# A convolution and gated feed-forward kernel: the opening's filter band, convolution order and two requests for x rearranged

## The chip, the core and the metric

The kernel runs on one core of a Trainium2 chip. A core has a matrix engine (TensorE, PE in the profile; its weight loads have rows of their own, PEld), a vector engine (VectorE, DVE), a scalar engine (ScalarE, ACT), a general engine (GpSimd, POOL) and a sync engine (SyncE, SP), which here issues transfers only. Each runs its own stream of instructions in order, and they meet at semaphores. TensorE writes its products into an accumulation memory, PSUM, in banks of 512 float32 columns; VectorE and ScalarE bring them from there to the working memory. The metric is device time in microseconds (us) for one execution.

## The reference

```python
def _attn_ref(x, weight):                       # x: 8 x 4096 x 192, weight: 8 heads x 7 taps
    w = np.exp(weight - np.max(weight, axis=-1, keepdims=True))
    w = w / (np.sum(w, axis=-1, keepdims=True) + 1e-09)
    x_pad = np.concatenate([np.zeros((B, pad, D)), x], axis=1)      # 6 zero rows in front
    ...
    out = np.einsum('hk,bskhg->bshg', w, x_unf)   # each head's 24 columns, 7 rows back
def _moe_ref(x, w_gate, w_val, w_out):          # 192 -> 1536 -> 192, on 32768 rows
    gate = np.maximum(x @ w_gate, 0.0)
    val = x @ w_val
    return gate * val @ w_out
```

A causal convolution over the sequence, with seven softmax taps per head, feeds a feed-forward layer whose hidden vector is the product of a rectified gate and a value.

## The kernel before

The 32768 rows are two streams of four sequences each, carried side by side. A unit is 2 x 512 rows of both streams, and there are 16 units. For each unit, `gate_val` (matmuls at L621) multiplies the convolved rows (`xc`, columns in three chunks `c` of 64) with `Wg` and `Wv` in twelve blocks `f` of 128 hidden columns; ScalarE rectifies the gate (L632) and VectorE multiplies by the value (L633). `project_turn` (L643) multiplies with `Wo`. From unit 1 on the convolution is done tap by tap on ScalarE, VectorE and GpSimd, a unit ahead. The first windows cannot wait for that, so the opening convolves them on TensorE with a band matrix. The order of every engine's stream is the order in which the code is written.

This opening is what the change touches. In the order of the code:

- `hold` (L193) issues matmuls of constant ones into the PSUM tile `held`; their results are not used. `WARM` gives their lengths in units of 128 columns: four at the start, three after the small matmul that spreads the taps (L203).
- The filter band. `spread` gets the taps, ScalarE and VectorE form the softmax, and VectorE writes `blocks` at L299: one scaled 22-column block for each of the 8 heads, in three instructions for heads 0 to 2, 3 to 5 and 6 to 7 (the three `BANDS`). TensorE (L335) places eight shifted copies of the blocks into PSUM with the shift matrix `Z`, eight matmuls for each band, all accumulating on zeros that L209 wrote there. VectorE casts the three bands to `band0`, `band3`, `band6` (L343). The third band's PSUM home is the second bank of `held`.
- Meanwhile the five steps of the first x window (`raw`, five transfers) are cast on ScalarE (L119), in the order `STEPS0` = 1, 0, 2, 3, 4.
- The first convolution (`conv_steps`, L391): for each chunk `c` and each step eight small matmuls in four 32-column tiles of the array, 120 in all, into three PSUM tiles `first[0..2]`. Chunk 0 reads `band0`, chunk 1 `band0` and `band3`, chunk 2 `band3` and `band6`.
- `evict` (L402) casts each chunk's 512 columns into `xc`: chunk 0 and 2 on ScalarE, chunk 1 on VectorE. `both_halves` (L231) copies a 128-column piece of a weight to the other 64 partitions: pieces 0 and 1 on VectorE, pieces 2 to 9 on GpSimd (`pool_halves`, a `Wg` and a `Wv` copy for each), piece 10 by transfer.
- GpSimd's stream also issues the transfers of the weights (L224) and of x. The x of the second window (`load_x(1, ...)`, L97) is asked for one stream at a time: stream 0 after piece 2, stream 1 after piece 5. It is used by `conv_steps(1, ...)` in block `f` = 10 of the first window.

Of the kernel before, what the change touches and what calls it, by code (L numbers as in the profile page):

```python
# [11 lines left out]
ALU = mybir.AluOpType  # L12
# [3 lines left out]
def kernel(  # L16
# [12 lines left out]
    nc = tc.nc  # L29

    B, S, D = x.shape
    H, KW = weight.shape
# [7 lines left out]
    WIN = 512  # L40
    NWIN = S // WIN
    SUB = 112
    STEP = 106
    STEPS = [6, 5, 2]
    TAPS = [(6, 5), (4, 3), (2, 1, 0)]
    GSUB = 5
    WARM = [(4, 4, 4, 1), (4, 4, 1)]
    STEPS0 = [1, 0, 2, 3, 4]
    CONV1 = 10


# [29 lines left out]
    def staged(i, j):  # L81
        return stages[i][:, XH * j : XH * (j + 1)]

    def load_x(g, streams=range(2)):


        bp, toks = GROUPS[g]
        xt = staged(g // 3, g % 3).rearrange("p (j s d) -> p j s d", s=2, d=D)
        step = toks[1] - toks[0]
        rows = -(-(step + PAD) // 16) * 16  # L90
        for st in streams:
            src = bass.AP(
                tensor=x.tensor,
                offset=x.offset + ((bp + NB * st) * S + toks[0] - PAD) * D,
                ap=[[D, rows], [step * D, len(toks)], [1, D]],
            )
            nc.gpsimd.dma_start(out=xt[0:rows, 0 : len(toks), st, :], in_=src)  # L97
        return xt

    xts = {0: staged(0, 0).rearrange("p (j s d) -> p j s d", s=2, d=D)}  # L100
# [56 lines left out]
    Z = const.tile([128, 256], F16)  # L157
    nc.gpsimd.memset(Z[:], 0.0)
    nc.gpsimd.memset(raw[0][0:PAD, :], 0.0)
    mask = const.tile([128, H, 1], FP)  # L160
    with nc.allow_low_precision("one of the terms is not zero"):
        nc.vector.tensor_reduce(
            out=Z[:, 112 : 112 + HR],
            in_=eye[:].rearrange("p (g i) -> p i g", i=HR),
# [4 lines left out]
        out=mask[:, :, 0],  # L169
        in_=eye[:].rearrange("p (g i) -> p g i", i=HR),  # L170
# [17 lines left out]
    def many(n):  # L188
        return bass.AP(tensor=one.tensor, offset=one.offset, ap=[one.ap[0], [0, n]])

    def hold(*counts):
        for reps in counts:
            nc.tensor.matmul(  # L193
                out=held[:, 0, 0 : 128 * reps],
                lhsT=many(128),
                rhs=many(128 * reps),
                start=True,
                stop=True,
            )

    spread = psum.tile([128, 2, 512], FP, name="ps")
    hold(*WARM[0])
    nc.tensor.matmul(out=spread[:, 0, 0:KW], lhsT=rows8[:], rhs=w8[:], start=True, stop=True)  # L203
# [25 lines left out]
    def both_halves(copy, s, dst):  # L229
        cols = slice(HALVES[s], HALVES[s + 1])  # L230
        copy(out=dst[64:128, :, cols], in_=dst[0:64, :, cols])  # L231
# [39 lines left out]
    for s in range(2):  # L271
# [4 lines left out]
        out=mx[:], in_=spread[:, 0, 0:KW], axis=mybir.AxisListType.X, op=ALU.max, negate=True  # L276
    )
    nc.scalar.activation(out=e[:, 0:KW], in_=spread[:, 0, 0:KW], func=ACTF.Exp, bias=mx[:])
    sm = const.tile([128, 1], FP)
    total = const.tile([128, KW + 1], FP)  # L280
    nc.scalar.activation(out=total[:], in_=e[:], func=ACTF.Copy, accum_out=sm[:])
    for jj in STEPS0[:3]:
        cast(nc.scalar.copy, jj)
# [4 lines left out]
        out=prod[:],  # L288
        in0=bass.AP(tensor=z0.tensor, offset=z0.offset, ap=[z0.ap[0], [1, BW], [1, KW]]),
        in1=bass.AP(tensor=e0.tensor, offset=e0.offset, ap=[e0.ap[0], [0, BW], [1, KW]]),  # L290
        op=ALU.mult,
    )
    blk = const.tile([128, 1, BW], FP)
    nc.vector.tensor_reduce(out=blk[:, 0, :], in_=prod[:], axis=mybir.AxisListType.X, op=ALU.add)
    nc.vector.reciprocal(sm[:], sm[:])
    blocks = const.tile([128, H, BW], F16)
    for heads in BANDS:
        n = len(heads)
        nc.vector.scalar_tensor_tensor(  # L299
            out=blocks[:, heads[0] : heads[0] + n, :],  # L300
            in0=blk[:].to_broadcast([128, n, BW]),
            scalar=sm[:],
            in1=mask[:, heads[0] : heads[0] + n, :].to_broadcast([128, n, BW]),
            op0=ALU.mult,
            op1=ALU.mult,
        )
# [4 lines left out]
    for s in range(2, 4):  # L311
        load_w(s)
    pool_halves(2)
    xts[1] = load_x(1, range(1))
    for s in (3, 4, 5):
        pool_halves(s)
    load_x(1, range(1, 2))
    for s in (6, 7):
        pool_halves(s)
# [3 lines left out]
    lane_load(0, range(1, 2))  # L323
    for jj in STEPS0[3:]:
        cast(nc.scalar.copy, jj)

    bands = [const.tile([128, len(heads), SUB], F16, name=f"band{heads[0]}") for heads in BANDS]
    for part, heads, to, copy in zip(
        raised, BANDS, bands, [nc.vector.tensor_copy] * 3
    ):  # L330
        n = len(heads)
        for j in range(128 // HR):
            s0 = HR * j - PAD
            lo, hi = max(0, -s0), min(BW, SUB - s0)
            nc.tensor.matmul(  # L335
                out=part[:, 0 : SUB * n].rearrange("p (h t) -> p h t", t=SUB)[:, :, s0 + lo : s0 + hi],
                lhsT=Z[:, 112 - HR * j : 240 - HR * j],
                rhs=blocks[:, heads[0] : heads[0] + n, lo:hi],
                start=False,
                stop=(j == 128 // HR - 1),  # L340
                skip_group_check=True,
            )
        copy(out=to[:].rearrange("p h t -> p (h t)"), in_=part[:, 0 : SUB * n])  # L343

    tap = const.tile([128, NCH, KW], FP)

    for c in range(NCH):
        r0 = 0
        while r0 < 64:
            h = (64 * c + r0) // G  # L350
            r1 = min(64, G * (h + 1) - 64 * c)
            row = wn[HR * h : HR * h + 8, :]
            for st in range(2):
                nc.sync.dma_start(
                    out=tap[64 * st + r0 : 64 * st + r1, c, :],
                    in_=bass.AP(
                        tensor=row.tensor,
                        offset=row.offset,
                        ap=[row.ap[0], [0, (r1 - r0) // 8], [1, KW]],
                    ),  # L360
# [6 lines left out]
    def band(h):  # L367
        return bands[h // 3][0 : SUB + PAD, h % 3, :]

    dense, xcs = {}, {}  # L370
# [6 lines left out]
    def conv_steps(g, ps, c, steps):  # L377


        for jj in steps:  # L380
            col = STEP * jj
            n = min(STEP, WIN - col)
            rows = n + PAD
            for second in range(2):
                for st in range(2):
                    for k2 in range(2):
                        k = 2 * c + k2
                        h0, h1 = 32 * k // G, (32 * k + 31) // G
                        h, m = (h0, G * h1 - 32 * k) if second else (h1, 32)
                        p0 = 64 * st + 32 * k2  # L390
                        nc.tensor.matmul(  # L391
                            out=ps[p0 : p0 + m, 0, col : col + n],
                            lhsT=xts[g][0:rows, jj, st, 32 * k : 32 * k + m],
                            rhs=band(h)[0:rows, 0:n],
                            start=True,
                            stop=True,
                            tile_position=(0, p0),
                            skip_group_check=True,
                        )

    def evict(copy, g, ps, c):
        copy(out=dense[0][:, g, c, :], in_=ps[:, 0, :])  # L402

    def conv(g):

# [301 lines left out]

    dense[0] = xcpool.tile([128, 2, NCH, WIN], F16, name="xc")
    first = [psum.tile([128, 2, 512], FP, name="ps") for _ in range(NCH)]
    for c, steps in ((0, STEPS0[:3]), (1, STEPS0[:2]), (0, STEPS0[3:]), (1, STEPS0[2:]), (2, STEPS0)):  # L710
        conv_steps(0, first[c], c, steps)
    both_halves(nc.vector.tensor_copy, 0, Wg)
    both_halves(nc.vector.tensor_copy, 0, Wv)
    for c, copy in enumerate((nc.scalar.copy, nc.vector.tensor_copy, nc.scalar.copy)):
        evict(copy, 0, first[c], c)
    both_halves(nc.vector.tensor_copy, 1, Wg)
    both_halves(nc.vector.tensor_copy, 1, Wv)
    xts[2] = load_x(2)
# [3 lines left out]
        out=plain.rearrange("p (c d) -> p c d", d=D), in_=moe_w_out.rearrange("(c p) d -> p c d", p=128)  # L722
# [78 lines left out]
```

## Time and profile before

| | |
|---|---|
| three timed runs | 761.57, 761.65, 763.04 us; median 761.65 |
| span of the profiled execution, first to last instruction | 760.2 us |
| TensorE busy | 756.0 us, 99% of the span |
| VectorE, ScalarE, GpSimd busy | 89%, 80%, 61% |
| first matmul of L621 | 7.81 us after the start |

The profiled execution has no time of its own in the list beside its span; against the median of the three runs, 1.4 us lie outside the span, before the first and after the last instruction. Rows of the profile give start and duration in us, then engine, line, operation, tile written and tiles read. A matmul's row is longer than the time after which the next can follow, since matmuls are pipelined. A number `x24` counts instructions that follow each other in one row, whose duration then runs from the first start to the last end.

### The profile page before, as it was taken

The page shows a single profiled execution, that of the slowest core. Times are in us where ns is not written, and L with a number is a line of the kernel's source. Part 1 is how long each engine was busy: PE and PEld are TensorE (multiplying, and loading weights), DVE is VectorE, ACT ScalarE, POOL GpSimd, SP SyncE. Part 2 cuts the span into 40 slices and gives each one's busy share as a digit, 9 for nine tenths or more (in the row PEclk, how much of TensorE's full clock was granted, in tenths as well). Part 3 has the DMA queues.
Part 4 walks back from the last instruction along what each step waited for, and adds up shares of the span by engine and source line. Part 5 has one row for each costly group of instructions (what it writes and reads, how often), then busy time and mean ns, then how long its engine had stood idle before and what let it go on. Part 6 is the DMA issues. An engine that isn't in the chain of part 4 may idle for free.

```text
span 760.2 us, 30531 instructions
## 1 busy us (share of the span) xinstructions
PE 756.0 (99%) x13724; PEld 454.8 (60%) x13724; DVE 675.8 (89%) x647; ACT 610.1 (80%) x680; POOL 461.3 (61%) x311
## 2 busy tenths in 40 slices
PE   9999999999999999999999999999999999999998
PEld 5555555565565666656666565666656556566658
DVE  7889989998998989989999899998999989897891
ACT  7897887878878788887877878788797887877671
POOL 8729649195591946829377392874919659193600
PEclk9999999999999999999999999999999999999999
DMA  8953532345324443333434324352243531240302
GB/s 142 137 69 92 79 85 46 43 96 75 85 44 52 97 66 85 55 61 83 60 85 71 66 67 55 85 85 69 56 49 93 77 86 44 23 100 9 85 2 85
DMA packets 153714, 54.07 MB, mean 71 GB/s; under 512 B 148912, under 2 KB 153584, under 8 KB 153584
## 3 DMA queue, kind: packets, MB, share of 16 engines
q1 hardware_dynamic: 117376, 37.78, 21.6%
q0 software_dynamic: 35808, 14.07, 16.4%
q8 instruction: 107, 1.75, 1.0%
q10 hardware_dynamic: 400, 0.27, 0.1%
q14 instruction: 23, 0.19, 0.1%
HBM read 28.98 MB, written 25.17 MB: 71 GB/s over the span
## 4 chain that ended last, share of the span: by engine, by line
PE 99%; DMA 0%; ACT 0%; issue 0%
PE ps L621 65%; PE ps L643 31%; PE ps L686 2%; PE ps L391 0%; DMA w<-in_weight_dram 0%; PE ps L193 0%; PE ps L335 0%; PE ps L414 0%; PE ps L209 0%; PE ps L203 0%; ACT out_s L697 0%; ACT L127 0%
## 5 line engine op out<-in xcount | busy, mean ns | idle before, releaser
L633 DVE TENSOR_TENSOR hT<-gr,ps 128x1024 f16<-128x1024 f16 (+1 forms) x385 | 469.1, 1219 | 35.5 <-ACT gr L632 8.7
L632 ACT ACTIVATE gr<-ps 128x1024 f16<-128x1024 f32 (+1 forms) x385 | 392.8, 1021 | 114.4 <-PE ps L621 114.4
L550 POOL TENSOR_TENSOR prod<-prod,prod 128x896 f32<-128x896 f32 x145 | 302.6, 2087 | 251.8 <-DVE prod L584 242.7
L621 PE MATMUL ps<-xc,Wg 64*64 64x512 f16 (+1 forms) x4464 | 318.4, 376 | 0.0
L621 PE MATMUL ps<-xc,Wv 64*64 64x512 f16 (+1 forms) x4464 | 318.3, 376 | 0.0
L643 PE MATMUL ps<-hT,Wo 64*64 64x512 f16 x4320 | 235.8, 376 | 0.0
L621 PEld LDWEIGHTS <-Wv 64*64 64x64 f16 (+1 forms) x4464 | 149.9, 106 | 98.5 <-DVE hT L633 0.3
L621 PEld LDWEIGHTS <-Wg 64*64 64x64 f16 (+1 forms) x4464 | 145.4, 107 | 103.4 <-issue 0.2
L643 PEld LDWEIGHTS <-Wo 64*64 64x64 f16 x4320 | 137.3, 107 | 95.7
L538 ACT ACTIVATE prod<-x_r,tap 128x1024 f32<-128x1024 f16 (+2 forms) x195 | 182.7, 1017 | 0.0
L574 DVE SCALAR_TENSOR_TENSOR acc<-x_r,tap,acc 128x1024 f32<-128x1024 f16 (+3 forms) x150 | 118.0, 854 | 0.0
L661 DVE STREAM_TRANSPOSE out_s<-ps 128x1024 f32<-128x1024 f32 x45 | 56.2, 1248 | 28.4 <-PE ps L643 24.4
L550 POOL TENSOR_TENSOR xc<-prod,prod 128x896 f16<-128x896 f32 x29 | 60.6, 2089 | 2.3
L479 POOL COPY x_p<-x_e 128x1536 f16<-128x1536 f16 (+1 forms) x32 | 42.2, 1351 | 0.0
L251 POOL DMA_DIRECT2D x_e<-in_x_dram x30 | 26.6, 890 | 0.0
L574 DVE SCALAR_TENSOR_TENSOR xc<-x_r,tap,acc 128x1024 f16<-128x1024 f16 (+3 forms) x30 | 25.2, 840 | 0.0
L563 ACT ACTIVATE acc<-x_r,tap 128x1024 f32<-128x1024 f16 (+3 forms) x30 | 22.5, 800 | 0.0
L656 ACT COPY turned_by<-ps 128x2 f32<-128x2 f32 x45 | 7.0, 155 | 16.8 <-PE ps L643 14.8
L686 PEld LDWEIGHTS <-hT 128*128 128x128 f16 x192 | 15.8, 98 | 0.4 <-issue 0.4
L686 PE MATMUL ps<-Wo,hT 128*128 128x192 f16 x192 | 16.0, 246 | 0.0
L697 ACT COPY out_s<-ps 128x768 f32<-128x768 f32 (+2 forms) x5 | 3.2, 638 | 12.7 <-PE ps L686 12.7
L697 DVE COPY out_s<-ps 128x192 f32<-128x192 f32 x1 | 0.4, 359 | 13.3 <-PE ps L686 13.3
(61 smaller groups left out, 74.4 us busy)
## 6 DMA issues: line engine op xcount, KB each, us to landing
out_dram<-out_s SPq DMA_DIRECT2D x125, 192.0 KB
x_e<-in_x_dram POOLq DMA_DIRECT2D x28, 384.0 KB, 6.3
x_r<-x_p SPq DMA_TRANSPOSE x116
prod<-in_moe_w_out_dram POOLq DMA_DIRECT2D x1, 576.0 KB, 8.7
prod<-in_x_dram SPq DMA_DIRECT2D x3, 168.0 KB
out_dram<-out_s SPq DMA_DIRECT2D x5, 96.0 KB
out_s<-in_x_dram POOLq DMA_DIRECT2D x2, 210.0 KB, 6.2
out_s<-in_x_dram POOLq DMA_DIRECT2D x2, 192.0 KB, 6.1
```

Source lines behind the costliest of these rows:

```text
L251: nc.gpsimd.dma_start(out=xe[:, 0:n, st, :, :].rearrange("p j c r -> p j (c r)"), in_=bass.AP(tensor=x.tensor, offset=x.offset + row * D, ...
L479: nc.gpsimd.tensor_copy(out=xp[:, js, :, st, :], in_=xe[:, js, st, :, :])
L538: nc.scalar.activation(out=both(prods[b, k], b, at, n), in_=shifted(b, c, k, t, n), func=ACTF.Copy, scale=tap[:, c, k : k + 1],)
L550: nc.gpsimd.tensor_tensor(out=acc if k < KW - 1 else xcs[b][:, w, :, :].rearrange("p c t -> p (c t)")[:, LDVE : NCH * WIN], in0=acc, in1=p ...
L563: nc.scalar.activation(out=both(accs[b], b, at, n), in_=shifted(b, c, 0, t, n), func=ACTF.Copy, scale=tap[:, c, 0:1],)
L574: nc.vector.scalar_tensor_tensor(out=result(b, at, n) if k == KW - 1 else both(acc, b, at, n), in0=shifted(b, c, k, t, n), scalar=tap[:, c ...
L621: nc.tensor.matmul(out=pss[i][q : q + M, st, :], lhsT=W[64 * st : 64 * st + 64, c, 128 * f + q : 128 * f + q + M], rhs=xcb[64 * st : 64 * ...
L632: nc.scalar.activation(out=gr[:, sts], in_=pss[0][:, sts], func=ACTF.Relu)
L633: nc.vector.tensor_tensor(out=h[:, f, sts], in0=gr[:, sts], in1=pss[1][:, sts], op=ALU.mult)
L643: nc.tensor.matmul(out=ps[64 * st : 64 * st + 64, b, :], lhsT=Wo[64 * r : 64 * r + 64, f, p, :], rhs=hs[b][64 * r : 64 * r + 64, f, st, :] ...
L661: nc.vector.transpose(out=o[:].rearrange("p t (b d) -> p b t d", b=2)[:, :, :, 32 * p : 32 * p + 32], in_=ps[:].rearrange("p b (t c) -> p ...
L686: nc.tensor.matmul(out=ps[:, i // 2, D * (i % 2) : D * (i % 2) + D], lhsT=h[:, f, st, 128 * q : 128 * (q + 1)], rhs=Wo[:, f, :, :].rearran ...
```

## The change

The `WARM` lengths change: the fourth `hold` matmul of the first group has 384 instead of 128 columns, and a third group of 512 and 256 columns is written behind the three band casts. The scaling of `blocks` becomes one instruction over all 8 heads. The band matmuls write 32 partitions each instead of 128, in four column tiles of the array, in the order `PLACED`. The convolution order of the first window changes: steps 1, 0, 2, 3 of chunk 0, the same of chunk 1, then step 4 of chunk 0, step 4 of chunk 1, then chunk 2. Chunks 0 and 1 are evicted in two parts: columns 0 to 317 (`early_cols`) and 318 to 511 (`late_cols`); chunk 0's early part stands on VectorE ahead of the copies of piece 0, its late part on ScalarE, chunk 1's early part on ScalarE and its late part on VectorE. Both requests of the second window's x stand behind the copies of pieces 3, 4 and 5 on GpSimd.

```diff
-    WARM = [(4, 4, 4, 1), (4, 4, 1)]
+    WARM = [(4, 4, 4, 3), (4, 4, 1), (4, 2)]
     STEPS0 = [1, 0, 2, 3, 4]
+    PLACED = [0, 2, 4, 6, 1, 3, 5, 7]
...
-    for heads in BANDS:
-        n = len(heads)
-        nc.vector.scalar_tensor_tensor(
-            out=blocks[:, heads[0] : heads[0] + n, :],
...
+    nc.vector.scalar_tensor_tensor(
+        out=blocks[:],
+        in0=blk[:].to_broadcast([128, H, BW]),
+        scalar=sm[:],
+        in1=mask[:].to_broadcast([128, H, BW]),
...
     pool_halves(2)
-    xts[1] = load_x(1, range(1))
     for s in (3, 4, 5):
         pool_halves(s)
+    xts[1] = load_x(1, range(1))
     load_x(1, range(1, 2))
...
-        for j in range(128 // HR):
+        for j in PLACED:
+            q = HR * j // 32 * 32
...
-                lhsT=Z[:, 112 - HR * j : 240 - HR * j],
+                lhsT=Z[:, 112 - HR * j + q : 144 - HR * j + q],
...
-                stop=(j == 128 // HR - 1),
+                stop=(j % 2 == 1),
+                tile_position=(0, q),
...
         copy(out=to[:].rearrange("p h t -> p (h t)"), in_=part[:, 0 : SUB * n])
+    hold(*WARM[2])
...
-    for c, steps in ((0, STEPS0[:3]), (1, STEPS0[:2]), (0, STEPS0[3:]), (1, STEPS0[2:]), (2, STEPS0)):
+    for c, steps in ((0, STEPS0[:4]), (1, STEPS0[:4]), (0, STEPS0[4:]), (1, STEPS0[4:]), (2, STEPS0)):
         conv_steps(0, first[c], c, steps)
+    early_cols, late_cols = slice(0, 3 * STEP), slice(3 * STEP, WIN)
+    evict(nc.vector.tensor_copy, 0, first[0], 0, early_cols)
     both_halves(nc.vector.tensor_copy, 0, Wg)
     both_halves(nc.vector.tensor_copy, 0, Wv)
-    for c, copy in enumerate((nc.scalar.copy, nc.vector.tensor_copy, nc.scalar.copy)):
-        evict(copy, 0, first[c], c)
+    evict(nc.scalar.copy, 0, first[0], 0, late_cols)
+    evict(nc.scalar.copy, 0, first[1], 1, early_cols)
+    evict(nc.vector.tensor_copy, 0, first[1], 1, late_cols)
+    evict(nc.scalar.copy, 0, first[2], 2)
```

On TensorE, from the end of the band matmuls to the first convolution; `ps_120` is `held`, `ps_243` is `first[0]`, and a name in brackets is the engine whose count the instruction waits for. Before:

```order
L335 MATMUL ps_120<-blocks_153,Z_110 128x2x22
L335 LDWEIGHTS Z_110
L335 MATMUL ps_120<-blocks_153,Z_110 128x2x6
L391 LDWEIGHTS out_s_84 [waits Activation_49]
L391 MATMUL ps_243<-band0_188,out_s_84 32x106 [waits DVE_49]
L391 LDWEIGHTS out_s_84
```

And now:

```order
L335 MATMUL ps_120<-blocks_153,Z_110 32x2x22
L335 LDWEIGHTS Z_110
L335 MATMUL ps_120<-blocks_153,Z_110 32x2x6
L194 LDWEIGHTS const-bfloat16-1.0
L194 MATMUL ps_120<-const-bfloat16-1.0 128x512 [waits DVE_49]
L194 LDWEIGHTS const-bfloat16-1.0
L194 MATMUL ps_120<-const-bfloat16-1.0 128x256
L395 LDWEIGHTS out_s_84 [waits Activation_49]
L395 MATMUL ps_243<-band0_186,out_s_84 32x106
```

The wait for VectorE stood at the first convolution matmul and stands now at the new `hold` matmul, whose tile is the one that the third band's cast reads; the convolution's matmuls have none of their own left.

On VectorE, from the casts of the bands to the first product of unit 0; `ps_244` is `first[1]`. Before:

```order
L343 CAST band0_188<-ps_130 128x336 [waits PE_49]
L343 CAST band3_189<-ps_131 128x336 [waits PE_49]
L343 CAST band6_190<-ps_120 128x224 [waits PE_49]
L231 COPY Wg_116<-Wg_116 64x3x128 [waits DMASW0_49]
L231 COPY Wv_117<-Wv_117 64x3x128 [waits DMASW1_49]
L402 CAST xc_242<-ps_244 128x512 [waits PE_49]
```

And now:

```order
L346 CAST band0_186<-ps_130 128x336 [waits PE_49]
L346 CAST band3_187<-ps_131 128x336 [waits PE_49]
L346 CAST band6_188<-ps_120 128x224 [waits PE_49]
L406 CAST xc_242<-ps_243 128x318 [waits PE_49]
L232 COPY Wg_116<-Wg_116 64x3x128 [waits DMASW0_49]
L232 COPY Wv_117<-Wv_117 64x3x128 [waits DMASW1_49]
L406 CAST xc_242<-ps_244 128x194 [waits Activation_49]
```

Chunk 0's early part stands ahead of the two copies, and chunk 1's late part waits for ScalarE where the whole chunk waited for TensorE.

On ScalarE, from the last cast of x to the first rectified gates; `ps_245` is `first[2]`. Before:

```order
L119 CAST out_s_84<-prod5_90 96x384 [waits DMAHW4_49]
L402 CAST xc_242<-ps_243 128x512 [waits PE_49]
L402 CAST xc_242<-ps_245 128x512 [waits PE_49]
L632 ACTIVATE gr_433<-ps_419 128x512 [waits PE_49]
L632 ACTIVATE gr_436<-ps_419 128x512
```

And now:

```order
L120 CAST out_s_84<-prod5_90 96x384 [waits DMAHW4_49]
L406 CAST xc_242<-ps_243 128x194 [waits DVE_49]
L406 CAST xc_242<-ps_244 128x318 [waits PE_49]
L406 CAST xc_242<-ps_245 128x512 [waits PE_49]
L636 ACTIVATE gr_435<-ps_421 128x512 [waits PE_49]
```

Chunk 0's late part waits for VectorE, which reads the same PSUM tile, and chunk 1's early part has come in between.

More of the change, by code (lines that the diff above doesn't have):

```diff
@@ L296 @@
     blocks = const.tile([128, H, BW], F16)
-    for heads in BANDS:
-        n = len(heads)
-        nc.vector.scalar_tensor_tensor(
-            out=blocks[:, heads[0] : heads[0] + n, :],
[L301 to L306, printed above, removed]
+    nc.vector.scalar_tensor_tensor(
[3 more added lines that the diff above has]
+        in1=mask[:].to_broadcast([128, H, BW]),
+        op0=ALU.mult,
+        op1=ALU.mult,
+    )
     wn = const.tile([128, KW], FP)
@@ L335 @@
             nc.tensor.matmul(
-                out=part[:, 0 : SUB * n].rearrange("p (h t) -> p h t", t=SUB)[:, :, s0 + lo : s0 + hi],
-                lhsT=Z[:, 112 - HR * j : 240 - HR * j],
+                out=part[q : q + 32, 0 : SUB * n].rearrange("p (h t) -> p h t", t=SUB)[
+                    :, :, s0 + lo : s0 + hi
+                ],
+                lhsT=Z[:, 112 - HR * j + q : 144 - HR * j + q],
                 rhs=blocks[:, heads[0] : heads[0] + n, lo:hi],
                 start=False,
-                stop=(j == 128 // HR - 1),
+                stop=(j % 2 == 1),
+                tile_position=(0, q),
                 skip_group_check=True,
@@ L399, in conv_steps, with evict @@
                         )
-    def evict(copy, g, ps, c):
-        copy(out=dense[0][:, g, c, :], in_=ps[:, 0, :])
+    def evict(copy, g, ps, c, cols=slice(0, WIN)):
+        copy(out=dense[0][:, g, c, cols], in_=ps[:, 0, cols])
     def conv(g):
```

## The prediction

> **What bounds the kernel now.** I read first the busy shares, then the chain that ended last in order of time, then the timeline of each engine in the opening. (Times and runs of this kernel tell a difference of about 0.2%, 1.52 us, from none.)
>
> ```profile
> PE 756.0 (99%) x13724; PEld 454.8 (60%) x13724; DVE 675.8 (89%) x647; ACT 610.1 (80%) x680; POOL 461.3 (61%) x311
> ```
> ```profile
> 5.14 1.05 PE ps L335 x24
> 6.19 1.61 PE ps L391 x120
> ...
> 7.81 13.22 PE ps L621 x120
> 21.03 1.64 PE ps L391 x120
> ```
> ```profile
> 9.13:20.85 11.72, 11.72 (x110) 6.07 (x106) 10.47 (x10) 9.59 (x11) 10.56 (x20) 1.00 1.02 136
> ```
>
> The chain is TensorE nearly from start to end, so from the first gate matmul at 7.81 on a delay of TensorE goes to the end one to one, unless a later stall absorbs it. The window from block f=1 to the second convolution shows how much could be absorbed: nine blocks of six pairs at 0.215 us are 11.6 us, and 11.72 went by. I allow at most 0.1 us and count none. So the change is worth what it does to the time at which block f=0 ends, 9.13.
>
> That time is set by a chain over three engines:
>
> ```profile
> 4.63 0.67 DVE L299 SCALAR_TENSOR_TENSOR blocks<-blk,sm,mask 128x66 f16<-128x66 f32 x3
> 5.56 1.22 DVE L343 CAST band<-ps 128x336 f16<-128x336 f32 x3 [0.26 <-PE ps L335]
> 6.81 0.39 DVE L231 COPY Wg<-Wg 64x384 f16<-64x384 f16 x1
> 7.02 0.32 DVE L231 COPY Wv<-Wv 64x384 f16<-64x384 f16 x1
> 7.44 0.69 DVE L402 CAST xc<-ps 128x512 f16<-128x512 f32 x1
> ```
> ```profile
> 4.97 0.83 PE L335 MATMUL ps<-blocks,Z 128*128 128x48 f16 x13
> ...
> 5.56 0.51 DVE L343 CAST band<-ps 128x336 f16<-128x336 f32 x1 [0.26 <-PE ps L335]
> ```
> ```profile
> 6.12 0.28 PE L391 MATMUL ps<-band,out_s 112*32 112x106 f16 x8
> ```
> ```profile
> 7.17 0.58 ACT L402 CAST xc<-ps 128x512 f16<-128x512 f32 x1 [0.48 <-PE ps L391]
> 8.06 0.58 ACT L402 CAST xc<-ps 128x512 f16<-128x512 f32 x1 [0.30 <-PE ps L391]
> ```
> ```profile
> 7.81 0.39 PE L621 MATMUL ps<-xc,Wg 64*128 64x512 f16 x2
> 8.02 0.39 PE L621 MATMUL ps<-xc,Wv 64*128 64x512 f16 x2
> 8.24 0.40 PE L621 MATMUL ps<-xc,Wg 64*128 64x512 f16 x2
> ...
> 8.70 0.39 PE L621 MATMUL ps<-xc,Wg 64*128 64x512 f16 x2
> ...
> 9.13 0.40 PE L621 MATMUL ps<-xc,Wg 64*128 64x512 f16 x2
> ```
>
> The first cast ends at 6.07 and the convolution starts at 6.12: it needs the first band alone, and the other two casts run beside it. ScalarE's eviction of chunk 0 ends at 7.75 and the gate starts at 7.81. Chunks 1 and 2 come at 8.13 (7.44 + 0.69) and 8.64 (8.06 + 0.58), just as the gate reaches them at 8.24 and 8.70. A hand-over from VectorE or ScalarE to TensorE thus costs 0.05 us.
>
> **The change part by part.** Durations by shape:
>
> ```profile
> L299 DVE SCALAR_TENSOR_TENSOR blocks<-blk,sm,mask 128x66 f16<-128x66 f32 x2 | 0.5, 292 | 0.0
> ...
> L299 DVE SCALAR_TENSOR_TENSOR blocks<-blk,sm,mask 128x44 f16<-128x44 f32 x1 | 0.3, 252 | 0.0
> ```
> ```profile
> L343 DVE CAST band<-ps 128x336 f16<-128x336 f32 x2 | 0.9, 502 | 0.3 <-PE ps L335 0.3
> L402 DVE CAST xc<-ps 128x512 f16<-128x512 f32 x1 | 0.7, 692 | 0.1
> ...
> L343 DVE CAST band<-ps 128x224 f16<-128x224 f32 x1 | 0.4, 380 | 0.0
> ```
> ```profile
> L632 ACT ACTIVATE gr<-ps 128x1024 f16<-128x1024 f32 x383 | 391.9, 1023 | 114.0 <-PE ps L621 113.9
> ```
> ```profile
> L632 ACT ACTIVATE gr<-ps 128x512 f16<-128x512 f32 x2 | 1.1, 594 | 0.5 <-PE ps L621 0.5
> ```
>
> *One scaling.* From 44 to 66 columns costs 40 ns, 1.8 ns a column; the casts grow by 1.09 (380 to 502 over 112). For 176 columns that bounds the instruction by 0.41 and 0.49 us; I take 0.45, since the form is its own but fixed costs are in both. It ends at 4.63 + 0.45 = 5.08, and the first band matmul, now at 4.97, starts at 5.13. This is a loss of 0.16 us there.
>
> *Tiles.* The 24 band matmuls take 1.05 us, 44 ns each; the first eight hold the first cast until 5.56, 0.59 after 4.97. Four tiles side by side make two rounds of eight, and would save at best three quarters of 0.35 us. At worst they go on one by one and save nothing. The convolution's rows, also four 32-column tiles, go 120 in 1.49 us (first start 6.12, last about 7.61), 12 ns each against 44 for 106 columns, so I take the best: the first cast at 5.13 + 0.59 - 0.26 = 5.46, bounds 5.46 to 5.72. The gain on the first cast is 0.1 us. The casts themselves are then VectorE's bound: 1.22 us in a row, the last done at 6.68.
>
> *The third hold.* Its first matmul waits for VectorE, and the convolution rows behind it no longer do; it writes the tile that the third cast reads. So it starts at 6.68 + 0.05 = 6.73, not in the hole that the shorter band matmuls leave, and the whole convolution is queued behind it on TensorE, with the evictions waiting for that. It streams 768 columns: 0.32 us at 0.215 for 512 (pairs at 7.81 and 8.02). Then the change of array tiling:
>
> ```profile
> 20.20 0.83 PE L621 MATMUL ps<-xc,Wv 64*128 64x512 f16 x6
> 20.96 0.33 PE L391 MATMUL ps<-band,out_s 112*32 112x106 f16 x12
> ```
>
> Three pairs from 20.20 stream until 20.85, and the convolution's first matmul starts at 20.96: 0.1 us. The convolution starts at 7.15, where it started at 6.12. The Trainium skill (TensorEngine Tiling (Array Packing), Key Properties) says that a change of tiling mode, not of tile, drains the engine; these rows agree, and the full-width hold between two tiled stages makes two such changes more. Without the drain the sum would be 0.1 us smaller.
>
> *The late step last, evictions in two parts.* The early cast of chunk 0 reads a tile whose step 4 now comes after chunk 1's four steps. Its wait is on TensorE's count for the tile, so I take it to start only after 72 convolution matmuls, 71 x 12 ns = 0.85 us, plus 0.24 us: the second convolution's chunk 0 has its 40 matmuls issued by 21.49 (20.96 + 39 x 1.64/120) and its eviction started here:
>
> ```profile
> 21.73 0.58 ACT L402 CAST xc<-ps 128x512 f16<-128x512 f32 x1 [0.29 <-PE ps L391]
> ```
>
> So VectorE starts at 7.15 + 0.85 + 0.24 = 8.24; 318 columns are 0.48 us (502 less 18 x 1.09): 8.72. ScalarE's late part waits for VectorE: 0.04 later, 194 columns at 0.58 - 318 x 0.84 ns (1023 less 594, over 512) = 0.32: 9.08. The gate starts at 9.13, 1.32 us after 7.81. Chunk 1's early part on ScalarE follows at about 8.98 (its instructions overlap by 0.1) and takes 0.42: 9.40; VectorE's late part waits for it, 9.44 + 0.35 = 9.79; TensorE gets chunk 1 at 9.84, where it would be ready at 9.13 + 0.43 = 9.56. Chunk 2 from ScalarE is done by 9.30 + 0.58 = 9.88, ahead of 9.84 + 0.43. Block f=0 ends at 9.84 + 0.86 = 10.70 against 9.13: **a loss of 1.57 us**. The two copies of piece 0, behind the early part on VectorE, end near 9.2, ahead of the pairs that need them within some hundredths; their old cover, the convolution, is gone.
>
> *The first hold.* 256 columns more, 0.21 us even at half speed, fall into a wait of TensorE for the transfer of the taps, 0.4 us long by the list of waits, and cost nothing:
>
> ```profile
> PE ps L203 <- DMA w<-in_weight_dram: 0.4, 1, 0.4
> ```
>
> *The requests of x.* GpSimd's stream:
>
> ```profile
> 9.34 0.86 POOL L97 DMA_DIRECT2D out_s<-in_x_dram  x1
> ...
> 11.49 0.50 POOL L231 COPY Wv<-Wv 64x384 f16<-64x384 f16 x1 [0.79 <-DMA Wv<-in_moe_w_val_dram]
> ...
> 13.74 0.79 POOL L97 DMA_DIRECT2D out_s<-in_x_dram  x1
> 14.53 0.52 POOL L231 COPY Wg<-Wg 64x384 f16<-64x384 f16 x1
> ```
> ```profile
> 17.68 0.52 POOL L231 COPY Wg<-Wg 64x384 f16<-64x384 f16 x1
> ```
> ```profile
> out_s<-in_x_dram POOLq DMA_DIRECT2D x2, 210.0 KB, 6.2
> ```
>
> The copy at 11.49 waits for its transfer whatever stands before it, so the copies of pieces 3 to 5 end when they did; from 13.74 on two requests stand where one stood, and everything behind is 0.86 us later, less the 0.37 or so that the next `Wv` copy waits anyway. Piece 8 would be copied by 18.7 instead of 18.2; block f=8 now starts at 18.26 and will start 1.5 us later. Stream 1's x, asked for at about 14.6, lands by 21 after 6.2 us, and the second convolution wants it at 20.96 + 1.5. Both are hidden by TensorE's delay; without it the copies would cost up to 0.5 us.
>
> **Sum.** 760.2 + 1.57 = 761.8 for the span; the median of the runs lies 1.45 above the span, so 761.65 + 1.57 = 763.2 us, slower by 0.21%.
>
> **Rivals.**
>
> *The hand-over is early (not slower).* If VectorE's early part of chunk 0 can start when steps 1, 0 and 2 are there, as the split into columns suggests, it starts 40 matmuls sooner, 0.48 us, and the serial evictions move up with it: +1.1 us, 762.7, within 0.2%. For it: the reorder leaves that gap. Against it: a single wait on TensorE's count stands there. It decides once the gate's first matmul comes before about 9.05.
>
> *The clock rises late (slower still).*
>
> ```profile
> L193 PE MATMUL ps<-const-bfloat16-1.0 128*128 128x512 bf16 x4 | 2.0, 614 | 0.8 <-PEq L785 0.8
> L621 PE MATMUL ps<-xc,Wg 64*64 64x512 f16 (+1 forms) x4464 | 318.4, 376 | 0.0
> ```
>
> A 512-column matmul takes 614 ns in the first 3 us and 376 later: TensorE starts at half speed and reached full speed somewhere before the convolution. The change leaves it idle from about 5.5 to 6.73. If the full speed then comes only after the convolution, the hold costs 0.32 more and 72 matmuls 0.85 more: 763.2 + 1.2 = 764.4. For it: the hole. Against it: the engine is busy for most of the time from 2.76 to 5.5. The Trainium skill (TensorE: Matmul & The Clock Gate, Part 1) says that full speed follows a busy window of some 3.4 us, that the windows run freely, and that the moment varies from run to run; the rows agree with a rise at about 6, and the 1.4 us between the runs would fit.
>
> *x lands late.* If the second stream's x is served after the first and lands, say, 0.8 us after it is wanted, the time is 764.0; the 1.5 us in hand at its usual 6.2 us speak against it.
>
> **How the numbers follow.** The sum as worked out 0.46 (763.2, its own range 762.9 to 763.6 from the bounds of the scaling, the rounds and the absorbed 0.1, a little more than half of it above 763.17), the early hand-over 0.23, the late clock 0.22, late x 0.04, and 0.05 for a gain that the profile does not show, such as the runs' 1.4 us of spread ending on the good side. Slower 0.30 + 0.22 + 0.04, about 0.56; within 0.2% 0.39; faster 0.05. The range goes from the early hand-over to beyond the late clock: 762.4 to 764.7.
>
> **What would show it.** The third hold's first row right after the third cast, near 6.7, with TensorE idle since about 5.5; the convolution at 7.15; VectorE's 318-column cast after 8.1; ScalarE's 194-column cast after it; the gate at 9.13 and chunk 1's matmuls with a hole of 0.3 us; everything from block f=1 on shifted by one constant. I am wrong if the hold starts by 6.1, if the evictions overlap, or if the convolution's matmuls go at 24 ns each.

## The result and the profile after

The changed kernel took 764.65 us (median of 7 runs, 764.24 to 765.18). The kernel before, run beside it again, took 762.53 (7 runs, 761.57 to 763.04). The ratio is 1.0029, with a 95% interval of 1.0019 to 1.0039: slower by 0.3%, 2.1 us. The three runs that the prediction started from had a median 0.9 us below that of the longer series; in the experiments below the kernel before had medians from 762.34 to 762.51. The forecast of 763.2 us was slower by 1.57 us than its base, so the loss was larger than forecast by about 0.6 us, and the rest of the distance from 763.2 to 764.65, 0.9 us, is the base.

The chain of the changed kernel, in order of time, from the tap transfer to the second convolution; rows are start, duration, engine and line:

```profile
0.88 2.08 DMA w<-in_weight_dram
...
5.76 1.23 DVE band L346 x3
...
7.03 0.80 PE ps L194 x2
7.83 1.71 PE ps L395 x72
...
9.57 0.50 DVE xc L406
...
10.09 0.66 ACT xc L406 x2
...
10.77 0.37 DVE xc L406
...
11.18 12.76 PE ps L625 x116
```

And its timelines of TensorE and of VectorE in the same stretch (rows left out where marked; what stands in brackets is the idle time before the row and what ended it):

```profile
5.41 0.48 PE L335 MATMUL ps<-blocks,Z 128*32 128x48 f16 x24
7.03 0.80 PE L194 MATMUL ps<-const-bfloat16-1.0 128*128 128x512 bf16 x2 [1.14 <-DVE band L346]
7.76 2.52 PE L395 MATMUL ps<-band,out_s 112*32 112x106 f16 x120
10.46 0.43 PE L625 MATMUL ps<-xc,Wg 64*128 64x512 f16 x2 [0.19 <-ACT xc L406]
10.68 0.43 PE L625 MATMUL ps<-xc,Wv 64*128 64x512 f16 x2
11.18 0.39 PE L625 MATMUL ps<-xc,Wg 64*128 64x512 f16 x2
...
12.04 0.40 PE L625 MATMUL ps<-xc,Wg 64*128 64x512 f16 x2
```
```profile
4.96 0.40 DVE L298 SCALAR_TENSOR_TENSOR blocks<-blk,sm,mask 128x176 f16<-128x176 f32 x1
5.76 1.22 DVE L346 CAST band<-ps 128x336 f16<-128x336 f32 x3 [0.40 <-PE ps L335]
9.57 0.49 DVE L406 CAST xc<-ps 128x318 f16<-128x318 f32 x1 [2.59 <-PE ps L395]
...
10.77 0.36 DVE L406 CAST xc<-ps 128x194 f16<-128x194 f32 x1
```

Where TensorE alone carried the chain before, it now runs over VectorE, back to TensorE, and twice over VectorE and ScalarE. TensorE stands idle for 1.14 us until the third band cast is done; the third hold follows at once (5.76 + 1.23 = 6.99, then 7.03). The hold writes the first bank of `held` and the cast reads the second, so the wait goes by the whole tile and not by the bank. Block f=1 starts at 12.04 instead of 9.13, and the second convolution and everything behind it keep that distance but for 0.15 us: the span grew from 760.2 to 762.9. Of the 2.9 us, 0.33 belongs to this execution, whose tap transfer landed that much later (TensorE's tap matmul at 3.09 instead of 2.76). The convolution, queued behind the hold, took 2.52 us for its 120 matmuls instead of 1.6.

### The profile page after: what moved, and what is told of

Its sections match the earlier page's. It is cut to its first block, busy times and chain, and to the rows that moved or that the text cites. A ratio compares the mean times of both kernels' runs of the same rounds, so it can differ in the third digit from the quotient of the medians.

```text
span 762.9 us, 30535 instructions
## 1 busy us (share of the span) xinstructions
PE 757.3 (99%) x13726; PEld 426.1 (56%) x13726; DVE 676.3 (89%) x646; ACT 610.7 (80%) x681; POOL 461.4 (60%) x311
## 4 chain that ended last, share of the span: by engine, by line
PE 99%; DVE 0%; DMA 0%; ACT 0%; issue 0%
PE ps L625 65%; PE ps L647 31%; PE ps L690 2%; PE ps L395 0%; DMA w<-in_weight_dram 0%; PE ps L194 0%; DVE band L346 0%; PE ps L418 0%; DVE xc L406 0%; PE ps L210 0%; ACT xc L406 0%; PE ps L204 0%; ACT out_s L701 0%; PE ps L335 0%; ACT L128 0%
## 5 line engine op out<-in xcount | busy, mean ns | idle before, releaser
L625 PE MATMUL ps<-xc,Wg 64*64 64x512 f16 (+1 forms) x4464 | 314.4, 376 | 0.3 <-ACT xc L406 0.2
L625 PE MATMUL ps<-xc,Wv 64*64 64x512 f16 (+1 forms) x4464 | 314.4, 376 | 0.0
L625 PEld LDWEIGHTS <-Wv 64*64 64x64 f16 (+1 forms) x4464 | 143.6, 106 | 105.1 <-DVE hT L637 0.3
L625 PEld LDWEIGHTS <-Wg 64*64 64x64 f16 (+1 forms) x4464 | 133.9, 107 | 115.1 <-issue 0.4
L647 PEld LDWEIGHTS <-Wo 64*64 64x64 f16 x4320 | 126.3, 107 | 106.7
```

Source lines behind the costliest of these rows:

```text
L625: nc.tensor.matmul(out=pss[i][q : q + M, st, :], lhsT=W[64 * st : 64 * st + 64, c, 128 * f + q : 128 * f + q + M], rhs=xcb[64 * st : 64 * ...
L647: nc.tensor.matmul(out=ps[64 * st : 64 * st + 64, b, :], lhsT=Wo[64 * r : 64 * r + 64, f, p, :], rhs=hs[b][64 * r : 64 * r + 64, f, st, :] ...
```

## The experiments

Three theories stood against each other. Theory 1: the third hold waits for the third cast, which keeps the convolution back and leaves TensorE idle, and the idle time also puts off TensorE's full speed; the evictions in two parts add a smaller loss. Theory 2: the moment of full speed is drawn by lot, whatever TensorE does. Theory 3: the evictions are the loss. The moment is read from TensorE's pace: the convolution's 120 matmuls take 1.6 us at full speed and 2.5 to 2.6 at half speed; a time in between means that the full speed came on the way. Differences of one kernel's median to another's carry the intervals of their ratios, about 0.09% or 0.7 us either way; where less than that is claimed, it is from the rows.

### The third hold taken out

```diff
-    hold(*WARM[2])
```

> The changed kernel without the third group of hold matmuls. Theory 1 (the third hold waits for the third cast, keeps the convolution back and leaves TensorE idle, and the idle time also puts off its full speed): the convolution starts right after the first cast, near 6.1 us, TensorE is idle for some 0.3 us only, the full speed comes at 6 to 7 us, and what is left is the serial evictions: 763.0 us, 0.5 over before, 1.6 under the changed kernel. Theory 2 (the moment of full speed is a matter of each run and has nothing to do with the hole): the convolution starts near 6.1 but at half speed until about 9.9, and the time is 764.0. Theory 3 (the evictions in two parts are the loss): no more than the hold's own 0.6 us comes back, 764.0, with the full speed early.

Measured: 763.08 us (11 runs), ratio to before 1.0008 (1.0000 to 1.0017). TensorE of this run:

```profile
5.93 2.00 PE L394 MATMUL ps<-band,out_s 112*32 112x106 f16 x120 [0.43 <-DVE band L346]
8.34 0.39 PE L624 MATMUL ps<-xc,Wg 64*128 64x512 f16 x2 [0.41 <-ACT xc L405]
```

The convolution starts behind the first cast again, a part of it at half speed, and 1.6 us of the 2.1 come back: theory 1's number. The gate still waits 0.41 us for ScalarE's part of chunk 0.

### The hold where no cast reads

```diff
-    hold(*WARM[2])
+    for reps in WARM[2]:
+        nc.tensor.matmul(
+            out=spread[:, 1, 0 : 128 * reps],
...
```

> The changed kernel with the third hold writing into the second bank of the tile that held the spread taps, which no cast reads any more, so that it waits for no band cast. Theory 1: the hold runs straight behind the band matmuls, 5.7 to 6.4 us, no hole is left, the convolution starts near 6.45, the full speed comes at 6 to 7 us: 763.2. Theory 2: full speed near 9.9 all the same: 764.3. Theory 3 (evictions): 763.9.

Measured: 762.90 us (11 runs, 762.24 to 763.56), ratio 1.0006 (0.9997 to 1.0015).

```profile
5.68 0.82 PE L348 MATMUL ps<-const-bfloat16-1.0 128*128 128x512 bf16 x2
6.43 2.20 PE L402 MATMUL ps<-band,out_s 112*32 112x106 f16 x120
9.05 0.47 PE L632 MATMUL ps<-xc,Wg 64*128 64x512 f16 x2 [0.42 <-ACT xc L413]
...
9.97 0.39 PE L632 MATMUL ps<-xc,Wg 64*128 64x512 f16 x2
```

The same matmuls, written one bank further on, now run straight behind the band and cost nothing that the ratio shows. So it is not the hold's work that costs, but whom it waits for.

### Convolution order and evictions as before, third hold left

```diff
-    for c, steps in ((0, STEPS0[:4]), (1, STEPS0[:4]), (0, STEPS0[4:]), (1, STEPS0[4:]), (2, STEPS0)):
+    for c, steps in ((0, STEPS0[:3]), (1, STEPS0[:2]), (0, STEPS0[3:]), (1, STEPS0[2:]), (2, STEPS0)):
...
-    evict(nc.vector.tensor_copy, 0, first[0], 0, early_cols)
...
+    for c, copy in enumerate((nc.scalar.copy, nc.vector.tensor_copy, nc.scalar.copy)):
+        evict(copy, 0, first[c], c)
```

> The changed kernel with the convolution order and the whole-chunk evictions of before; the third hold with its wait stays. Theory 1: TensorE is still idle from 5.7 to 7.0, full speed still near 9.9, the convolution still at half speed; the gate starts when chunk 0 (56 matmuls at 22 ns, then 0.6 us of eviction) is there: about 0.5 earlier than in the changed kernel, 764.1. Theory 3 (evictions are the loss): 762.7, as before.

Measured: 764.35 us, ratio 1.0025 (1.0016 to 1.0034). Two of the 11 runs took 762.5 and 762.6, the other nine 763.8 to 765.6. The profiled run is one of the nine.

```profile
6.65 0.80 PE L194 MATMUL ps<-const-bfloat16-1.0 128*128 128x512 bf16 x2 [1.14 <-DVE band L346]
7.38 2.53 PE L395 MATMUL ps<-band,out_s 112*32 112x106 f16 x120
9.84 0.39 PE L625 MATMUL ps<-xc,Wg 64*128 64x512 f16 x2
```

The wait, the 1.14 us of idle time and the convolution at half speed are all still there without the split evictions. Theory 3 falls. Why two runs were as fast as the kernel before stays open, since neither has a profile.

### The band alone

```diff
-    for heads in BANDS:
-        n = len(heads)
-        nc.vector.scalar_tensor_tensor(
...
+    nc.vector.scalar_tensor_tensor(
+        out=blocks[:],
...
-        for j in range(128 // HR):
+        for j in PLACED:
...
-                stop=(j == 128 // HR - 1),
+                stop=(j % 2 == 1),
+                tile_position=(0, q),
```

This is the kernel before with the one scaling and the 32-column tiles.

> The kernel before with the band alone changed: one scaling, 32-column tiles. Theory 1: first cast 0.1 us earlier, convolution 0.1 earlier, TensorE idle some 0.4 us ahead of it, full speed as before near 6 us: 762.4, no difference from before. A rival (matmuls in small tiles count less as work, so the full speed is put off by them): full speed near 9.5, convolution at half speed, 763.5 or more.

Measured: 762.75 us, ratio 1.0006 (0.9997 to 1.0015): no difference. The gate started early in the profiled run, at 7.64, and lost it again at block f=3. TensorE and GpSimd:

```profile
7.64 0.39 PE L624 MATMUL ps<-xc,Wg 64*128 64x512 f16 x2
```
```profile
13.04 0.82 PE L624 MATMUL ps<-xc,Wv 64*128 64x512 f16 x5 [0.18 <-POOL Wv L232]
```
```profile
12.48 0.50 POOL L232 COPY Wv<-Wv 64x384 f16<-64x384 f16 x1 [1.21 <-DMA Wv<-in_moe_w_val_dram]
```

The copy of that piece of `Wv` waited for its transfer and TensorE for the copy. A start before the old one thus has a limit of its own in the arrival of the weights. By the medians the tiles neither brought nor cost time that the interval shows; in this one profile they did not put the full speed off.

### The idle time filled, the wait left

```diff
+    for reps in (4, 4, 3):
+        nc.tensor.matmul(
+            out=spread[:, 1, 0 : 128 * reps],
...
     hold(*WARM[2])
```

> The changed kernel with 1408 more columns of hold matmuls into the spread tile ahead of the third hold: TensorE is kept busy from 5.7 to 7.0 us, but the third hold's wait for the third cast, and the start of the convolution behind it, stay where they are. This tells the wait from the idle time. Theory 1: the full speed comes before 8 us, the convolution goes at 12 ns a matmul for the most part, and the time is 763.8 (before plus the 1.3 to 1.6 us of waits). Theory 2 (full speed has nothing to do with the idle time): near 9.9 as in the changed kernel, 764.6.

Measured: 763.95 us (11 runs, 763.45 to 764.44), ratio 1.0020 (1.0011 to 1.0029).

```profile
5.23 0.77 PE L348 MATMUL ps<-const-bfloat16-1.0 128*128 128x512 bf16 x3
6.51 0.49 PE L194 MATMUL ps<-const-bfloat16-1.0 128*128 128x512 bf16 x2 [0.51 <-DVE band L346]
6.93 1.58 PE L403 MATMUL ps<-band,out_s 112*32 112x106 f16 x120
9.01 0.52 PE L633 MATMUL ps<-xc,Wg 64*128 64x512 f16 x2 [0.50 <-ACT xc L414]
...
9.98 0.39 PE L633 MATMUL ps<-xc,Wg 64*128 64x512 f16 x2
```

In the profiled run TensorE was at full speed before the fill ended, so 0.51 us of idle time was left; hold and convolution ran at full speed, 0.49 and 1.58 us, behind the same wait. This is the case that the prediction's sum described: it had the convolution at 7.15 and the gate at 9.13, and here, with the tap matmul 0.22 us earlier, they come at 6.93 and 9.01. Since the full speed was there before TensorE could idle, this profile shows what the wait costs at full speed, not what the idle time does to the moment of full speed. On that there are only the times: the 11 runs lie at 764.44 or below, the seven of the changed kernel at 764.24 or above.

### The convolution order and the evictions alone

```diff
+    evict(nc.vector.tensor_copy, 0, first[0], 0, early_cols)
     both_halves(nc.vector.tensor_copy, 0, Wg)
     both_halves(nc.vector.tensor_copy, 0, Wv)
...
+    evict(nc.scalar.copy, 0, first[0], 0, late_cols)
+    evict(nc.scalar.copy, 0, first[1], 1, early_cols)
+    evict(nc.vector.tensor_copy, 0, first[1], 1, late_cols)
```

The kernel before with these evictions and the convolution order of the change.

> The kernel before with the convolution order and the evictions in two parts alone. Theory 1: the convolution starts at 6.1 as before, VectorE's early part of chunk 0 starts only when step 4 of chunk 0 is done, the gate starts 0.4 us later than before and loses another 0.2 to 0.3 at chunk 1: 763.0, slower by 0.5. Rival (the split hands chunk 0 over early): 762.2 to 762.4.

Measured: 763.47 us, ratio 1.0009 (1.0000 to 1.0018); six of the 11 runs lie between 763.45 and 763.50, the others between 762.05 and 763.48. The chain of this run, and GpSimd's copies in the same stretch:

```profile
6.31 1.71 PE ps L391 x72
...
8.04 0.49 DVE xc L402
...
8.56 0.52 DVE Wg L231
9.09 0.46 DVE Wv L231
...
9.59 13.15 PE ps L621 x117
```
```profile
8.44 0.50 POOL L231 COPY Wg<-Wg 64x384 f16<-64x384 f16 x1
8.89 0.50 POOL L231 COPY Wv<-Wv 64x384 f16<-64x384 f16 x1
```

VectorE's early part of chunk 0 starts after 72 convolution matmuls, as the prediction had it; the early hand-over does not happen. The weight copies that it pushes back then fall beside GpSimd's two copies and take 0.52 us each (the chain shows 0.46 of the second, since they overlap). The kernel before has them ahead of GpSimd's, 0.39 and 0.32 us. The convolution of this run goes at half speed from start to end, though TensorE has next to no idle time between its tap matmul at 2.88 and the gate:

```profile
6.24 2.64 PE L391 MATMUL ps<-band,out_s 112*32 112x106 f16 x120
8.94 0.59 PE L621 MATMUL ps<-xc,Wg 64*128 64x512 f16 x2
```

So the 763.48 of this run holds the evictions and a late full speed together, and the full speed can come late without idle time ahead of the convolution; TensorE's one wait here, 0.48 us, is for the tap transfer.

### The third hold alone, twice, and with its idle time filled, twice

```diff
+    WARM = [(4, 4, 4, 1), (4, 4, 1), (4, 2)]
...
+    hold(*WARM[2])
```

> The kernel before with the third hold alone, which waits for the third cast here too. Theory 1: convolution 1.1 us later than before with full speed, gate 1.0 later, since chunk 0 is read by ScalarE in one piece: 763.5; where the idle 0.6 us puts off the full speed, 764.3. Rival (the hold fills a hole and costs nothing): 762.5.

> The kernel before with the third hold alone, a second time, beside the next run on the same chip. Theory 1 (the idle time in front of the third hold puts off the full speed in part of the runs): two groups of runs again, about half of them over 764.5. Theory 2 (the two groups were a matter of the chip or of the hour): one group, or as many over 764.5 as in the next run.

With 1024, then 1280 columns of hold into `spread` ahead of the third hold, which keeps its wait:

> The kernel before with the third hold and its wait alone, as in the run with that edit, and with 1024 more columns of hold into the spread tile ahead of it, so that the same wait stands in the same place but TensorE does not idle through it. Theory 1 (the idle time puts off the full speed): the runs with only the third hold fell into two groups, 762.9 to 763.3 and 765.0 to 765.7; here the upper group is gone, all runs are within 762.8 to 763.7. Theory 2 (the moment is drawn by lot whatever TensorE does): two groups again, 764 in the middle.

> The same with 1280 columns of hold into the spread tile ahead of the third hold, enough to fill the idle time at half speed too. Theory 1: all runs, or all but one, between 762.8 and 764.0, median 763.4. Theory 2: as many over 764.5 as in the run before.

Measured, all against the kernel before on the same chip:

| third hold alone, in the kernel before | median, ratio | runs under 764.4 | runs from 764.9 on |
|---|---|---|---|
| first time (6 runs) | 764.16, 1.0026 (1.0014 to 1.0039) | 762.93 to 763.31, three | 765.00 to 765.73, three |
| second time (11) | 764.99, 1.0022 (1.0010 to 1.0034) | 762.49 to 762.88, five | 764.99 to 765.86, six |
| filled, 1024 columns (11) | 763.48, 1.0014 (1.0005 to 1.0022) | 762.83 to 763.93, ten | 765.83, one |
| filled, 1280 columns (12) | 763.28, 1.0016 (1.0007 to 1.0025) | 762.45 to 764.32, ten | 765.81, two |

Where the runs fall in two groups, the median is a matter of one run more or less (in the second row it is the lowest of the upper group), and the ratio on record, 1.0022, is not that of the medians. The profiled executions of the first two are of the lower group. These are rows of the first, and the convolution of the last kernel, at 764.32:

```profile
6.92 0.51 PE L193 MATMUL ps<-const-bfloat16-1.0 128*128 128x512 bf16 x2 [0.64 <-DVE band L343]
7.35 1.60 PE L392 MATMUL ps<-band,out_s 112*32 112x106 f16 x120
```
```profile
8.16 2.13 PE L400 MATMUL ps<-band,out_s 112*32 112x106 f16 x120
```

With the full speed there (0.51 and 1.60 us), the lower group lies about 0.5 us above the kernel before. The upper group is 2 us above the lower. With the same wait and the idle time filled, 3 of 23 runs are in the upper group, where 9 of 17 were; of 123 runs of the kernel before, over all the series, one is over 764.4 (764.77). So the idle time makes times in the upper group far more frequent, and theory 2 falls in its strong form. That the upper group is the one with a late full speed is inferred: no run in it has a profile. And the idle time ahead of the third hold is not the only cause: in the profile of the last kernel TensorE idles nowhere between the tap matmul and the gate, and the convolution still takes 2.13 us. Which run is late remains a lottery, and filling the hole does not end it.

### Without either wait

```diff
-    hold(*WARM[2])
+    for reps in WARM[2]:
+        nc.tensor.matmul(
+            out=spread[:, 1, 0 : 128 * reps],
...
+    for c, copy in enumerate((nc.scalar.copy, nc.vector.tensor_copy, nc.scalar.copy)):
+        evict(copy, 0, first[c], c)
```

> The changed kernel with the hold moved to the spread tile and with the convolution order and evictions of before, so that both waits are gone and the band, the first hold and the requests stay changed. Theory 1: 762.6, no difference from before. If something else of the change costs time (requests, band), 763.0 or more; if the rest of the change is worth anything, under 762.2.

Measured: 762.40 us, ratio 1.0000 (0.9991 to 1.0009).

```profile
5.20 0.50 PE L348 MATMUL ps<-const-bfloat16-1.0 128*128 128x512 bf16 x2
5.77 1.68 PE L402 MATMUL ps<-band,out_s 112*32 112x106 f16 x120
7.42 0.39 PE L632 MATMUL ps<-xc,Wg 64*128 64x512 f16 x2
```

All of the loss is gone with the two waits, and nothing is gained by what remains of the change.

### The requests of x alone, and a longer first hold

```diff
-    xts[1] = load_x(1, range(1))
     for s in (3, 4, 5):
         pool_halves(s)
+    xts[1] = load_x(1, range(1))
```

> The kernel before with both requests of the second window's x behind the six copies, and nothing else. By the prediction's working: GpSimd's stream is up to 0.5 us later from the copies of piece 6 on, and the copy of piece 8 comes 0.2 to 0.4 us late for block f=8: 762.7 to 762.9. Rival: it is covered, 762.5.

Measured: 762.86 us, ratio 1.0002 (0.9993 to 1.0011): no difference that this tells.

```diff
-    WARM = [(4, 4, 4, 1), (4, 4, 1)]
+    WARM = [(4, 4, 4, 4), (4, 4, 1)]
```

> The kernel before with 512 instead of 128 columns in the last matmul of the first hold, so that TensorE has no hole before the tap transfer lands. Theory 1: a busy window can begin at 0.85 us already, the full speed comes by 4.3 to 7.7 us in every run, and the upper end of the runs of before (763.1) comes down: median 762.2, spread under 1 us. Rival: the hole there does nothing: 762.5 with the old spread.

Measured: 762.57 us (761.86 to 762.97), ratio 0.9999 (0.9990 to 1.0008). The expected gain did not come. The profiled run, at 762.76, had its full speed late, though TensorE's only idle time was 0.25 us ahead of the tap matmul:

```profile
6.33 2.46 PE L391 MATMUL ps<-band,out_s 112*32 112x106 f16 x120
```

```diff
-    WARM = [(4, 4, 4, 3), (4, 4, 1), (4, 2)]
+    WARM = [(4, 4, 4, 4, 1), (4, 4, 1), (4, 2)]
```

This last edit is on the kernel without either wait.

> The version without either wait (third hold in the spread tile, convolution order and evictions of before) with 640 columns in the last part of the first hold. Theory 1: full speed by 7.7 us in every run, the band is ready 0.3 us earlier than before, but the weights of block f=3 land no earlier: 762.1, a little under both kernels. Rival: 762.4, nothing gained, since the start of the gate is not what ends the first window then.

Measured: 762.44 us (762.15 to 763.33), ratio 1.0000 (0.9991 to 1.0009). No version beat the kernel before.

## Why the prediction fell short

**Right.** *The wait.* The third hold starts when the third cast is done, and the convolution stands behind it. With the hole filled, the convolution's first matmul comes 4.39 us after the tap matmul (6.93 less 2.54), as in the prediction (7.15 less 2.76), against 3.36 in the kernel before (6.12 less 2.76): 1.03 us. The medians, 763.95 with the hole filled and the wait left and 762.90 with the hold elsewhere, differ by 1.05, though medians tell no difference under 0.7 by themselves. *The evictions.* The split hands nothing over early; the early part waits for all of chunk 0 (72 matmuls) and the parts wait for each other: 9.57, 10.09, 10.77 in the chain. From VectorE's start to the gate it is 0.89 us (9.57 to 10.46), as forecast (8.24 to 9.13). The hole at chunk 1 is 0.29 us (10.68 to 11.18 less 0.215) where 0.28 was forecast. *The durations.* The 176-column scaling took 0.40 (0.45 taken, 0.41 the lower bound), the 318-column cast 0.49 (0.48), the 194-column cast on ScalarE 0.32 (0.32). The six rounds of band tiles started within 0.27 us, about a quarter of the 1.05 before, so the best case taken there was right. *No cost* for the first hold's extra columns and for the requests, which the runs agree with to 0.1%.

**Wrong.** The step that failed is the pace of the third hold and of the convolution behind it: 0.32 us for 768 columns and 12 ns a matmul, which is full speed. The profiled run shows half speed in its place; the other six have no profile, but lie within 0.6 us of it. From the hold's first matmul to the convolution's first it took 0.73 us (7.03 to 7.76) where 0.42 was forecast, drain included; from there to VectorE's early part it took 1.81 us (7.76 to 9.57) where 1.09 was forecast. These two terms were 1.03 us too small. Together with the 0.33 us of the later tap transfer they are, to 0.02 us, the distance from the forecast end of block f=0 at 10.70 to the measured one at 12.04; no other step of the sum is off by more than 0.05 us. The prediction had named 24 ns a matmul as a sign of being wrong, and 72 matmuls in 1.71 us are that.

The late clock was a rival with a chance of 0.22 and a price of 1.2 us, and the range reached 764.7 because of it; the sum's own range ended at 763.6. The row that should have weighed more was in the prediction's own text: TensorE idle from 5.5 to 6.73, in a kernel whose first 6 us are at half speed. How far the idle time is the reason for the half speed is shown by counts, not by a trace: filling it brings the median down by 0.7 us, and the share of the upper group from 9 in 17 to 3 in 23, but two kernels without idle time between the tap matmul and the convolution (the evictions alone, the longer first hold) had half speed as well, with 2.64 and 2.46 us for it. What sets the moment of full speed stays open. The medians of the experiments add up, 1.05 for the wait, 0.5 for the evictions (762.90 less 762.40) and 0.7 for the idle time, to 2.25 us against 2.1 measured; as each carries 0.7 us, that they close so well is luck.

The Trainium skill (TensorE: Matmul & The Clock Gate, Part 1) has full speed follow a busy window of 3.4 us, free-running, and calls the moment run-variable. The runs agree that the moment varies: the convolution took 1.6 to 2.6 us over the profiles, and one kernel's times fall in two groups 2 us apart. That times in the upper group become rarer when the idle time is filled fits a window that has to be busy; its length, and how much idle time it may hold, no run here settles.

**Also wrong:** the copies of piece 0, said to end some hundredths ahead of the pairs that need them, are what holds the profiled runs of three versions at 763.45 to 763.48 (below). In the changed kernel itself they come after GpSimd's pair and did not matter. And the base of 761.65 was a median of three runs from a series that spreads over 1.5 us. The prediction put it 1.45 us above the span of 760.2; in every later profiled run the time lies 1.67 to 1.82 us above the span (764.65 and 762.9 for the changed kernel), so the profiled execution of before stands for 761.9 to 762.0.

## What to carry to other kernels

A filler instruction is only free if nothing it touches is still being read: before adding one, look at who last reads the tile that it writes, since a tile that nobody reads any more gave 762.90 us where this one gave 764.65, though the cast read another bank of it. Splitting an eviction over two engines that read the same tile made a chain of them, not a pair. And at the start of a kernel an idle stretch of TensorE can be paid twice, once as a wait and once, in many runs, as half speed afterwards.

## What the runs showed that was not expected

VectorE's 64x384 copies take 0.27 to 0.39 us ahead of GpSimd's first pair of the same shape, and about 0.52 beside it, as at 8.56 and 8.44 in the run with the evictions alone. That pair starts at 8.44 to 8.47 in every profile and ends at 9.39 to 9.46, and a VectorE copy that begins while one of its copies runs ends some 0.14 us behind that copy wherever it began: in three kernels, from starts at 8.56, 8.63 and 8.68, the first of piece 0's copies ends at 9.08 or 9.09 and the second at 9.53. Chunk 1 is then ready at the same moment: in these kernels, whose starts are quite different (the hold in the spread tile, the hole filled, the evictions alone), the gate's chunk 1 begins at 9.97 or 9.98, and these three profiled runs took 763.45, 763.47 and 763.48 us. Five kernels have runs piled up within 0.13 us around 763.5; that the others share this cause is not shown. The Trainium skill (SBUF — State Buffer, SBUF: two separate sides) says that VectorE, in some of its modes, and GpSimd share a pair of ports as an exclusive lock, and that the loser blocks for the whole instruction; these rows agree.

Full speed is not a steady property of kernels close to the one before either: with the requests alone moved, the convolution took 2.10 us in the profiled run (762.86), and with the longer first hold 2.46 (762.76), where the profile before has 1.68. The 1.5 us between the fastest and the slowest of the first seven runs of before would fit the moment at which full speed comes, but no run at the upper end of that kernel's times has a profile.
